# Small TensorE tiles, a split inversion and one written order of issue in a DeltaNet and MLP-Mixer kernel

## The chip, the cores and the metric

The kernel runs on one core of one Trainium2 chip. Its time is the device time of one launch in microseconds. A profile is one such launch, taken on the same chip; its "span" runs from the first to the last instruction and is about 1.8 us shorter than the launch. TensorE's granted clock is printed as a share of full speed: 1.00, or 0.50 where it was halved.

## The reference

Four batch elements, eight heads, 768 positions, head width 48. The first part is a delta-rule recurrence, the second a mixer of two small MLPs, one across the positions and one across the channels:

```python
for t in range(S):
    y[:, :, t] = einsum('bhd,bhde->bhe', q[:, :, t], state)
    v_old = einsum('bhde,bhd->bhe', state, k_n[:, :, t])       # k_n: k / (|k| + 1e-6)
    state = state + beta_t * outer(k_n[:, :, t], v[:, :, t] - v_old)
# x: y as (batch, 768, 384)
u = x + (relu(x^T @ w_tok1) @ w_tok2)^T        # 768 -> 256 -> 768
out = u + relu(u @ w_ch1) @ w_ch2              # 384 -> 1536 -> 384
```

The weights come as float64 and are rounded to fp32 in the kernel.

## The kernel before

The recurrence is done in chunks of 64 positions, twelve per batch element; two chunks are a unit of 128 rows. For each unit and head a triangular 64x64 matrix has to be inverted. VectorE inverts its 32x32 diagonal blocks by substitution, for up to four units in one round, and TensorE joins the blocks:

```python
def invert(rnd):                       # 30 steps of two VectorE operations
    for s in range(1, HB - 1):         # HB = 32
        w = HB - 1 - s
        nc.vector.tensor_tensor(out=tmp, in0=x[:, 0:s, s:s+1]..., in1=x[:, s:s+1, s+1:HB]..., op=mult)
        nc.vector.tensor_tensor(out=x[:, 0:s, s+1:HB], in0=x[:, 0:s, s+1:HB], in1=tmp, op=add)
        yield
```

Each chunk is then three products that wait for one another, over two heads at a time as block-diagonal matrices of 128 rows. The zero halves make TensorE do twice the work, and each result is copied out in two halves:

```python
p_q = kqt[:, 2p+cc]^T @ s0[:, p]       # 128x128 by 96 columns
r_bd[r, :, e] = v_st - p_q             # VectorE, once per half
p_w = gm^T @ r_bd                      # 128x65 by 96
w_bd[r, :, e] = p_w                    # ScalarE, once per half
p_s = gm^T @ w_bd                      # 128x128 by 96
s1[r, :, e] = s0 + p_s                 # VectorE, once per half
```

Every piece of work is a generator, and a heap of (time, step) values decides in which order their steps are issued. Each engine carries out its own instructions in that order.

## Time and profile before

| stretch | us | what happens |
|---|---|---|
| A 0 to 39.5 | 39.5 | loads, preparation of the first units |
| B 39.5 to 86.0 | 46.5 | first round of inversion, on VectorE |
| C 86.0 to 96.6 | 10.6 | joining the blocks |
| D 96.6 to 180.6 | 83.9 | recurrence of the first batch element |
| 180.6 to 820.8 | 640.2 | four mixers and the other three recurrences |

The time was 821.29 us, the median of three runs (819.48 to 821.9). The lines behind the table are in the prediction. A stage ends where the timeline shows the event named, and its busy times are read for that stretch alone: 92% for TensorE over the whole span says nothing of B, where TensorE waits for VectorE.

### The profile page before, as it was taken

How to read it: one execution, taken by the hardware profiler on the slowest of the kernel's cores; microseconds unless marked ns; L12 is line 12 of the kernel's file. 1: busy time of each engine (PE TensorE's matmuls, PEld its weight loads, DVE VectorE, ACT ScalarE, POOL GpSimd, SP SyncE). 2: the span in 40 equal slices, each digit the busy share in tenths (PEclk: the TensorE clock that was granted, in tenths of full speed). 3: DMA queues.
4: the chain of work that ended last, by engine and by line, in shares of the span. 5: the costliest groups of instructions: out<-in, count | busy, mean ns of one | idle time of the engine just before them, and what ended most of it. 6: DMA issues, size and time to landing. Idle time of an engine off the chain costs nothing.

```text
span 820.8 us, 13554 instructions
## 1 busy us (share of the span) xinstructions
PE 753.4 (92%) x5204; PEld 611.7 (75%) x5204; DVE 411.8 (50%) x1115; ACT 266.9 (33%) x619; POOL 103.4 (13%) x126
## 2 busy tenths in 40 slices
PE   7772598898889999999999999999999999999998
PEld 4641576776669887876977889868888888578876
DVE  4699899868863576332394233762258221100000
ACT  4524545653425531332322333212322221011110
POOL 2043002424321200020100011010000000000000
PEclk9786699999999999999999999999999999999999
DMA  7536212465433332231313031121011100000000
GB/s 128 103 89 134 76 34 46 99 160 136 135 105 65 69 79 55 47 71 36 65 25 73 21 62 28 41 65 17 18 30 33 34 11 10 10 3 18 10 10 20
DMA packets 151088, 46.60 MB, mean 57 GB/s; under 512 B 142416, under 2 KB 145488, under 8 KB 151024
## 3 DMA queue, kind: packets, MB, share of 16 engines
q1 hardware_dynamic: 151024, 45.74, 25.2%
q8 instruction: 41, 0.67, 0.4%
q14 instruction: 23, 0.19, 0.1%
HBM read 36.27 MB, written 9.44 MB: 56 GB/s over the span
## 4 chain that ended last, share of the span: by engine, by line
PE 61%; DVE 22%; ACT 6%; DMA 4%; issue 4%; SPq 3%; POOL 1%; ACTq 0%; POOLq 0%; DVEq 0%
PE p_o L648 17%; PE p_c L632 16%; DVE sub L458 6%; PE p_g L367 5%; DVE x L462 5%; PE p_s L562 4%; PE p_q L530 3%; PE p_h L606 3%; PE p L593 3%; PE p_w L548 3%; PE p_z L487 2%; PE p_x L496 2%; ACT kbd L345 2%; SPq L272 2%; DMA kst<-in_k_dram 1%
## 5 line engine op out<-in xcount | busy, mean ns | idle before, releaser
L632 PE MATMUL p_c<-u_t,wc 128*128 128x128 f32 x1728 | 215.1, 278 | 2.7 <-ACT u_t L620 2.7
L632 PEld LDWEIGHTS p_c<-u_t,wc 128*128 128x128 f32 x1728 | 204.8, 193 | 8.0 <-ACT u_t L620 3.2
L648 PE MATMUL p_o<-wc,r 128*128 128x384 f32 x576 | 198.2, 490 | 5.9 <-DVE wc L207 5.9
L648 PEld LDWEIGHTS p_o<-wc,r 128*128 128x128 f32 x576 | 104.5, 190 | 69.2 <-DVE wc L207 9.6
L640 ACT ACTIVATE r<-p_c 128x512 f32<-128x512 f32 x72 | 43.0, 597 | 142.6 <-PE p_c L632 142.2
L458 DVE TENSOR_TENSOR sub<-x 128x30 f32<-128x30 f32 (+22 forms) x210 | 77.4, 369 | 12.7 <-DMA x<-n_dram 8.2
L462 DVE TENSOR_TENSOR x<-x,sub 128x30 f32<-128x30 f32 (+22 forms) x210 | 76.3, 363 | 4.0
L367 PE MATMUL p_g<-kqt,kbd 128*128 128x128 f32 x384 | 59.1, 309 | 18.1 <-ACT kqt L357 18.0
L654 DVE TENSOR_TENSOR xb<-xb,p_o 128x384 f32<-128x384 f32 x24 | 13.3, 555 | 121.0 <-PE p_o L648 120.8
L367 PEld LDWEIGHTS p_g<-kqt,kbd 128*128 128x128 f32 x384 | 53.8, 219 | 24.8 <-ACT kqt L357 23.5
L369 DVE TENSOR_TENSOR gm<-p_g,mb 128x512 f32<-128x512 f32 x48 | 33.0, 689 | 52.6 <-PE p_g L367 52.3
L566 DVE TENSOR_TENSOR s_bd<-s_bd,p_s 64x192 f32<-64x192 f32 (+1 forms) x100 | 31.6, 316 | 52.1 <-PE p_s L562 50.1
L562 PE MATMUL p_s<-w_bd,gm 128*128 128x96 f32 x384 | 54.4, 279 | 2.9 <-ACT w_bd L552 2.3
L536 ACT ACTIVATE xb<-p_q 64x384 f32<-64x384 f32 (+1 forms) x55 | 22.9, 419 | 103.3 <-DVE r_bd L532 99.2
L562 PEld LDWEIGHTS p_s<-w_bd,gm 128*128 128x128 f32 x384 | 48.4, 191 | 8.6 <-ACT w_bd L552 7.5
L532 DVE TENSOR_TENSOR r_bd<-v_st,p_q 64x192 f32<-64x192 f32 (+1 forms) x110 | 34.7, 316 | 38.8 <-PE p_q L530 24.7
L552 ACT COPY w_bd<-p_w 64x192 f32<-64x192 f32 (+1 forms) x120 | 33.5, 279 | 55.9 <-PE p_w L548 53.6
L530 PEld LDWEIGHTS p_q<-s_bd,kqt 128*128 128x128 f32 x352 | 45.2, 191 | 8.2 <-issue 2.2
L530 PE MATMUL p_q<-s_bd,kqt 128*128 128x96 f32 x352 | 48.3, 275 | 2.4 <-DVE s_bd L566 2.3
L156 PE MATMUL p_warm<-warm 128*128 128x256 f32 (+1 forms) x124 | 47.9, 511 | 1.5 <-DVE warm L98 1.1
L487 PE MATMUL p_z<-t,gm 128*65 128x64 f32 x384 | 28.5, 227 | 22.0 <-DVE t L482 21.9
L205 POOL TENSOR_TENSOR w_f<-w_f,d 128x384 uint32<-128x384 uint32 (+1 forms) x34 | 37.1, 1092 | 79.1 <-DVE w_f L199 35.6
(86 smaller groups left out, 779.0 us busy)
## 6 DMA issues: line engine op xcount, KB each, us to landing
d<-in_moe_w_ch_dram SPq DMA_DIRECT2D x24, 384.0 KB, 3.6
kpad<-in_k_dram SPq DMA_DIRECT2D x24, 192.0 KB, 3.2
kst<-in_k_dram SPq DMA_DIRECT2D x96, 48.0 KB, 2.7
qpad<-in_q_dram SPq DMA_DIRECT2D x24, 192.0 KB, 3.5
v_st<-in_v_dram SPq DMA_DIRECT2D x96, 48.0 KB, 2.6
out_dram<-xb SPq DMA_DIRECT2D x24, 192.0 KB, 1.9
n_dram<-gm SPq DMA_DIRECT2D x72, 32.0 KB, 1.7
gm<-w_dram SPq DMA_DIRECT2D x72, 32.0 KB, 2.1
```

What stands on the lines that cost most here:

```text
L156: nc.tensor.matmul(p, zero, zero[:, None, :].to_broadcast([128, m, 128]))
L205: nc.gpsimd.tensor_tensor(out=f, in0=f, in1=lo, op=ALU.add)
L367: nc.tensor.matmul(p_g[:, i], kbd[:, nb], kqt[:, nb])
L458: nc.vector.tensor_tensor(out=tmp, in0=x[:, 0:s, s : s + 1].to_broadcast([n, s, w]), in1=x[:, s : s + 1, s + 1 : HB].to_broadcast([n, s, w ...
L462: nc.vector.tensor_tensor(out=x[:, 0:s, s + 1 : HB], in0=x[:, 0:s, s + 1 : HB], in1=tmp, op=ALU.add,)
L487: nc.tensor.matmul(p_z[0 : C + 1, nb], weights_of(u, nb), t11[:, nb])
L530: nc.tensor.matmul(p_q[:, p], kqt[:, 2 * p + cc], s0[:, p])
L532: nc.vector.tensor_tensor(out=r_bd[r, hp, e], in0=v_st[r, hp, cc], in1=p_q[hi, hp, e], op=ALU.subtract,)
L562: nc.tensor.matmul(p_s[:, p], gm[:, 2 * p + cc, 0:2], w_bd[:, p])
L632: nc.tensor.matmul(p_c[:, i], piece_of(wc1, cb, f * 128)[:, f * 128 : (f + 1) * 128], u_t[:, cb], start=(cb == 0), stop=(cb == NCB - 1),)
L640: nc.scalar.activation(r, p_c, ACTF.Relu)
L648: nc.tensor.matmul(p_o, r2[f // FG][:, f % FG], piece_of(wc2, f, 0), start=(f == 0), stop=(f == NHT - 1),)
```

## The change

Its intent: the first batch element has nothing to overlap with until the mixer has an input, so everything ahead of the first mixer matmul counts. There are three parts. Blocks of 16 in place of 32 halve the steps of substitution, and TensorE joins them in 32-row tiles. The first recurrence works in 64-row tiles, each on a quarter of the array, so that no zero halves are multiplied or copied. The heap of times is replaced by one written list of 2,184 steps.

```diff
-        for s in range(1, HB - 1):
-            w = HB - 1 - s
+        for s in range(1, m - 1):              # m = 16 for the first batch element, k = 2 blocks at once
+            w = m - 1 - s
...
+    def join_16(u):                            # 32-row tiles
+        for nb in range(NB):
+            for i, (block, _, _) in enumerate(quarters(u)):
+                r = slice(HB * i, HB * i + HB)
+                nc.tensor.matmul(p_z[r, nb], block[:, nb], t16[r, :, j * NB + nb])
...
+    def recur_early(t):                        # 64-row tiles
+            for p, i in by_head:
+                nc.tensor.matmul(p_k[PAR[i], p], kqt[f, 2 * p + cc, 0], s0[f, p])
+            nc.vector.tensor_tensor(out=rest, in0=p_k, in1=v_st[:, :, cc], op=ALU.subtract)
+            ... p_y, p_w, a ScalarE copy, p_s, the new state, p_y again
...
-    at(*WEIGHTS[1], load_weights, (wc1, moe_w_ch1))     # and the rest of the plan of times
-    run_plan()
+    order = """
+    w1*5 w2 z x*2 b k0*4 w2 k0 x y*2 w2*3 p0*2 y p0 y*3 k0 k1 b*2 p0*7 k1*4 p1*2 w3 k1
+    ... (r: recurrence, i: inversion, j, h: joining, p: preparation, w: weights, m: mixer, x y z: warming)
+    """
+    for word in order.split():
+        name, _, n = word.partition("*")
+        for _ in range(int(n or 1)):
+            next(jobs[name])
```

## The prediction

> **What bounds the kernel now.** I read the page first, then busy time stage by stage, then the order of TensorE's work in time. The page:
>
> ```profile
> span 820.8 us, 13554 instructions
> PE 753.4 (92%) x5204; PEld 611.7 (75%) x5204; DVE 411.8 (50%) x1115; ACT 266.9 (33%) x619; POOL 103.4 (13%) x126
> PE   7772598898889999999999999999999999999998
> DVE  4699899868863576332394233762258221100000
> PEclk9786699999999999999999999999999999999999
> ```
>
> TensorE's 92% is an average over two regimes. From slice 12 on (about 240 us) it is full at full clock; before that VectorE is the fuller engine and TensorE's clock is throttled. So I cut the span at the events that the timeline shows: inversion of the first four units begins (39.46), ends (86), first recurrence matmul (96.64), first mixer matmul (180.58), last wait of the mixer for its weights (236.19), last mixer alone (704.19).
>
> ```profile
> 0.00:39.46 39.46, 29.63 (x169) 22.20 (x170) 21.11 (x56) 20.67 (x40) 4.44 (x18) 0.87 0.64 120
> 39.46:86.00 46.54, 21.07 (x76) 12.53 (x75) 44.81 (x111) 15.40 (x34) 16.78 (x20) 0.76 0.52 115
> 86.00:96.64 10.64, 5.96 (x36) 4.84 (x37) 10.07 (x28) 8.19 (x17) 0.00 (x0) 0.50 0.16 66
> 96.64:180.58 83.94, 75.39 (x606) 65.38 (x604) 70.75 (x229) 45.96 (x135) 20.56 (x21) 0.97 0.36 77
> 180.58:236.19 55.61, 47.12 (x234) 33.32 (x232) 49.51 (x130) 23.95 (x49) 23.12 (x22) 0.97 0.44 124
> 236.19:704.19 468.00, 461.65 (x3448) 387.27 (x3449) 208.34 (x552) 138.61 (x321) 38.49 (x45) 1.00 0.21 45
> 704.19:820.80 116.61, 112.60 (x642) 86.15 (x641) 7.21 (x13) 14.06 (x26) 0.00 (x0) 1.00 0.04 13
> ```
>
> Columns: stretch and length; busy time of matmul, weight load, VectorE, ScalarE, GpSimd; granted clock; DMA share; GB/s. VectorE is busy 44.8 of 46.5 us in the inversion, 10.1 of 10.6 while the blocks are joined, 70.8 of 83.9 in the recurrence. TensorE's 75.4 us in the recurrence includes 20.6 us of warming matmuls, which a query for their tile gives. TensorE's order:
>
> ```profile
> 33.32 3.54 PE L367 MATMUL p_g<-kqt,kbd 128*128 128x128 f32 x16 [2.46 <-ACT kqt L357]
> 65.18 2.05 PE L367 MATMUL p_g<-kqt,kbd 128*128 128x128 f32 x16 [1.46 <-ACT kqt L357]
> 88.25 1.99 PE L487 MATMUL p_z<-t,gm 128*65 128x64 f32 x16 [21.02 <-DVE t L482]
> 142.78 1.09 PE L548 MATMUL p_w<-r_bd,gm 128*65 128x96 f32 x8 [0.56 <-DVE r_bd L532]
> 144.14 1.20 PE L562 MATMUL p_s<-w_bd,gm 128*128 128x96 f32 x8 [0.27 <-ACT w_bd L552]
> 180.58 7.93 PE L593 MATMUL p<-xb,w 128*128 128x384 f32 x24
> 219.20 0.91 PE L648 MATMUL p_o<-wc,r 128*128 128x384 f32 x2 [0.76 <-DVE wc L207]
> ```
>
> TensorE waits 21 us for the inversion, then for a VectorE or ScalarE step between recurrence matmuls, and from 209 to 236 in short waits for VectorE's last weight conversions. Two regimes follow: up to the mixer's start the end is set by VectorE and the dependent chain, after that by TensorE's total work. A microsecond saved before 180 therefore counts, if no work is pushed behind it.
>
> **What the Trainium skill says.** (1) TensorEngine Tiling (Array Packing), section Tiling Modes: tiles work independently and can load weights and multiply in parallel, but changing the tiling mode drains the engine. The trace has one tiled group: beta's transposes, 32x64 tiles, two column groups:
>
> ```profile
> L166 PE MATMUL p_b<-ident,b_rows x48: 204/204/225, 9.6 to 10.9; 32*64 32x16 f32 x48
> 9.58 1.57 PE L166 MATMUL p_b<-ident,b_rows 32*64 32x16 f32 x48
> ```
>
> 48 passes in 1.57 us are 33 ns each, against 0.92/16 = 57 ns for a 65-column pass of joining (the chain's 0.92 us for 16). So concurrency agrees; the untiled matmuls behind it start without a visible gap, so a drain is not visible here. (2) TensorE: Matmul & The Clock Gate, Part 1: an idle window of about 3.4 us halves the clock. This agrees: granted 0.50 at 86 to 97, and 16 passes p_g take 3.54 us cold, 2.05 warm. (3) The same page, Part 2, LDWEIGHTS: loading goes by columns. This agrees: 65 columns 57 ns, 128 about 117 (eight p_s passes take 0.93 to 0.95). (4) SBUF — State Buffer, Who interferes with whom: a tensor_tensor with two SBUF inputs contends with GpSimd reads. This agrees: an 84-element multiply took 1.02 us beside a GpSimd operation, 0.24 without.
>
> **The change part by part.** An fp32 matmul is two passes here.
>
> *Inversion.* Now 60 VectorE operations per round by a mean of 0.366 us (L458, L462) = 22.0, plus transposes 2.0 + 1.9: 26 us. After: 14 steps of 2 operations on 28 to 112 elements, where forms of 30 to 108 elements take 0.21 to 0.35, say 0.27: 7.6; transposes 2.0 + 1.0 + 1.9, memsets 0.3: 13 us. There are two early rounds, so 26 us of VectorE work go.
>
> *Joining the 16-blocks* is added: per unit 64 + 64 passes of 32x32 tiles by 33 ns = 4.2 us of TensorE, one ScalarE copy, four small copies. Joining the 32-blocks becomes 64 passes by 33 ns = 2.1 us, before 0.94 + 0.92.
>
> *Recurrence.* Per chunk now on VectorE: 4 r_bd by 0.255, 4 s_bd by 0.256, 2 y by 0.347 = 2.7 us; after: one 128x192 and two 48x192 by 0.36 = 1.1, y goes to ScalarE. Over 12 chunks 20 us go. TensorE: 40 matmuls, 80 passes by 33 = 2.6 us, as before (8 by 117 + 8 by 83 + 8 by 117 ns = 2.5). The longest chain, three stages of 16 passes (0.53 + 0.25 latency), copies of 0.36, 0.36, 0.72 and three handovers of 0.2, is about 4.4 us per chunk; now 83.9/12 = 7.0.
>
> *Preparation.* Two ScalarE copies into kbd (0.58 each) go for six units: 7 us. p_g has 32 passes over two tiles, so about the same 1.8 us. The first weights are now loaded ahead of k, which delays k by about 2.5 us (three issues of 0.6 and their transfers).
>
> *Late batches.* p_s loads 112 columns rather than 128: 288 passes by about 14 ns = 4 us less TensorE. The rest stays.
>
> *The explicit order.* I counted the work in it between its own milestones, with the durations above:
>
> - A, to the start of inversion: VectorE 23.8, TensorE 12.5, ScalarE 17.0, 33 DMA issues of about 0.6 = 20. The last k lands near 22, plus one unit's chain, plus queueing behind weights: 32 us (before 39.5).
> - B, inversion: VectorE 14.8, little else; 18 us with GpSimd contention (before 46.5).
> - C, to the first recurrence matmul: TensorE 14.5, ScalarE 10.8, VectorE 7.4, but ten handovers: 15 us (before 10.6; this gets longer).
> - D, recurrence to the first mixer matmul: VectorE 74.6, TensorE 65.5, ScalarE 56. VectorE stays full: inversion of the second round (12), a third of the third round's (12), weights 18, preparation 14, recurrence 12. At the present 84 to 87% fill: 85 us (before 83.9). So D keeps its length, because work that came later is pulled into it.
>
> Mixer start: 32 + 18 + 15 + 85 = 150, against 180.6: 30 us earlier.
>
> After it, TensorE. Per mixer 116.6 us (the last one alone), four = 466. Per late unit now: preparation 2.7, joining 1.86, two chunks 4.95 = 9.5; 18 units 171; of that four preparations (11) lie ahead of 180.6, which leaves 626. Measured 820.8 - 180.6 = 640: 14 us are idle, which the waits from 196 to 236 account for. After the change I counted the order from its first mixer step on, operation by operation, at back-to-back rates (322 ns per 384-column pass, 112 per 128-column pass, 117 and 83 for late recurrence, 103 for the narrower p_s): 601 us. So counted, a mixer is 112 us, against 116.6 measured alone; the gaps of the first three are filled by other work, those of the last are not: 605. Idle time: VectorE still has 49 us until the last weight is converted, beside 52 us of TensorE work, the same ratio as now; I leave 11 us. Sum: 150 + 605 + 11 = 766.
>
> **The rivals.** *(a) Small tiles do not overlap.* With 32- or 64-row tiles at 57 ns per pass, or with drains at mode changes, the 2,100 tiled passes of recurrence and joining cost 24 ns more each, 50 us; half of it would be hidden behind VectorE: 790. For it: only one short tiled group is in the trace. Against: its 33 ns. *(b) Cold clock.* The order has almost no warming in the recurrence, and small tiles may not count as activity. At clock 0.5 a stage costs 0.5 us more, three stages in 12 chunks = 19 us, and preparation doubles: 785 to 795. For it: 0.50 at 86 to 97. Against: with 65 us of work in 85 the idle gaps stay short. *(c) One wrong place in a fixed order blocks an engine.* The order is long and fitted; if durations are off by 10%, queues wait for one another, costing 10 to 20 us: 780. *(d) The chain sets D, not VectorE:* 12 by 4.4 = 53 us, with TensorE's 65 as the floor: D 70, total about 750. *(e) No gain, since weights arrive at the same time:* conversions finish at 236 now; the order ends them about 60 us after the mixer starts, so near 210. DMA is 0.36 to 0.52 busy, so it can follow. That would have to fail for the time to stay near 810.
>
> **Range and chances.** (d) gives the low end, (a) and (b) the high end; together 745 to 792 should hold it 8 times in 10. For less than 2% gain (above 804.9) two rivals must come true at once: faster 0.93, same 0.05, slower 0.02.
>
> **What would show it right or wrong.** Inversion (28 operations, mean 0.27) over 18 us; VectorE in it still near full. First mixer matmul near 150. Tiled passes at about 33 ns start to start. Granted clock near 1 in the recurrence. Last weight conversion near 210. The last mixer alone still 116 us. The prediction is wrong if the mixer starts after 170, or if TensorE then shows more than 25 us of waits.

## The result

The changed kernel took 786.02 us, the median of four runs (783.87 to 786.98), against 820.38 (817.5 to 821.9) for the kernel before in the same rounds. The ratio is 0.9582, 95% interval 0.9547 to 0.9616. Such a ratio is the mean time of one kernel's fast runs over that of the other's in the same rounds, so it is not quite the ratio of the medians.

The page of the changed kernel, the lines that the prediction shows of before:

```profile
span 784.5 us, 16847 instructions
PE 742.1 (95%) x6950; PEld 607.9 (77%) x6950; DVE 383.0 (49%) x983; ACT 256.0 (33%) x589; POOL 99.5 (13%) x122
PE   8879987988899999997899999999999999999998
DVE  6987778898735724337433538231228433200000
PEclk9976568799999999999799999999999999999999
```

The clock line is the first surprise. Slices 3 to 7 (59 to 157 us) hold the recurrence, and the clock is low there while TensorE's own line shows 7 to 9. One more dip stands at slice 19, near 380 us. The stages, in the columns of the prediction's table:

```profile
0.00:29.00 29.00, 24.52 (x299) 17.86 (x299) 20.74 (x62) 16.09 (x34) 5.46 (x15) 1.00 0.77 160
29.00:47.00 18.00, 12.98 (x89) 7.02 (x93) 17.00 (x48) 5.49 (x11) 3.92 (x5) 1.00 0.63 129
47.00:61.16 14.16, 12.41 (x486) 10.33 (x486) 12.01 (x29) 9.49 (x23) 4.51 (x5) 0.62 0.47 108
61.16:148.67 87.51, 78.49 (x1758) 70.74 (x1755) 70.49 (x173) 50.93 (x125) 25.83 (x28) 0.69 0.46 99
148.67:212.00 63.33, 54.79 (x407) 42.04 (x405) 55.06 (x123) 32.47 (x73) 22.45 (x26) 1.00 0.51 127
212.00:667.90 455.90, 446.71 (x3279) 373.40 (x3278) 199.81 (x538) 126.36 (x294) 37.37 (x45) 0.99 0.21 44
667.90:784.50 116.60, 112.22 (x653) 86.51 (x651) 7.92 (x15) 15.16 (x29) 0.00 (x0) 1.00 0.04 13
```

| stretch | before | predicted | measured |
|---|---|---|---|
| A, to the inversion | 39.5 | 32 | 29.0 |
| B, first inversion | 46.5 | 18 | 18.0 |
| C, joining | 10.6 | 15 | 14.2 |
| D, recurrence of the first element | 83.9 | 85 | 87.5 |
| from the first mixer matmul on | 640.2 | 616 | 635.8 |
| span | 820.8 | 766 | 784.5 |

So 32 us are gained ahead of the mixer, where 30 were predicted, and 4 after it, where 24 were expected. Two things need explaining: the missing 20 us, and whether D is as long as predicted for the reason that was given, since the clock there was to be near 1.

In the timeline of TensorE one wait stands out in the later part. The lines are start, length, engine, line, operation, tiles, shapes and, in brackets, the idle time ahead and what ended it:

```profile
374.36 0.72 DVE L722 TENSOR_TENSOR r_bd<-p_q,v_st 64x192 f32<-64x192 f32 x2
375.12 0.48 ACT L726 COPY xb<-p_q 64x384 f32<-64x384 f32 x1 [11.55 <-DVE r_bd L722]
375.62 1.09 ACT L819 ACTIVATE r<-p_c 128x512 f32<-128x512 f32 x2
376.27 10.56 PE L827 MATMUL p_o<-wc,r 128*128 128x384 f32 x24 [8.26 <-ACT r L819]
```

The wait is named for the mixer's relu (L819), but the relu is only a bystander. It stands in ScalarE's queue behind the copy of L726, which stands behind VectorE's r_bd of the same p_q, and that comes after the steps of a late inversion. Each engine waits for its next instruction in the list, though later ones could go. The Trainium skill, TensorE: Matmul & The Clock Gate, Architectural detail, says that ScalarE and VectorE are strict first-in first-out queues; this trace agrees: ScalarE is idle for 11.55 us ahead of the copy, and the relu behind it starts at 375.62, though the p_c matmuls, the last of them at 367.68, had long ended. TensorE is idle for 8.26 us, its clock falls, and the 24 passes behind take 10.56 us rather than 24 by 0.322 = 7.7: together about 11 us.

To see the rest I counted TensorE's passes in each stretch at the back-to-back rates of the prediction. After the mixer's start they make 601.4 us, where 601 was predicted. The elapsed 635.8 us therefore hold 34.4 us of excess, against 15 allowed: 13.3 up to 212 us, while weights are still converted, 11.3 between 358 and 390 us around that wait, 5.2 in the last mixer, 4.6 spread over the rest.

### The profile page after: what moved, and what is told of

Its sections match the earlier page's. It is cut to its first block, busy times and chain, and to the rows that moved or that the text cites. A ratio compares the mean times of both kernels' runs of the same rounds, so it can differ in the third digit from the quotient of the medians.

```text
span 784.5 us, 16847 instructions
## 1 busy us (share of the span) xinstructions
PE 742.1 (95%) x6950; PEld 607.9 (77%) x6950; DVE 383.0 (49%) x983; ACT 256.0 (33%) x589; POOL 99.5 (13%) x122
## 4 chain that ended last, share of the span: by engine, by line
PE 79%; DVE 11%; SPq 3%; issue 2%; ACT 2%; DMA 2%; POOL 1%; POOLq 0%; ACTq 0%; DVEq 0%
PE p_o L827 24%; PE p_c L811 23%; PE p_g L385 4%; PE p_s L743 3%; PE p_q L719 3%; PE p L772 3%; DVE x L512 3%; PE p_w L735 3%; DVE sub L507 2%; SPq L292 2%; PE p_h L785 2%; PE p_z L604 2%; PE p_x L613 2%; PE p_t L353 1%; PE p_w L665 1%
## 5 line engine op out<-in xcount | busy, mean ns | idle before, releaser
L819 ACT ACTIVATE r<-p_c 128x512 f32<-128x512 f32 x72 | 42.9, 597 | 202.1 <-PE p_c L811 201.7
L833 DVE TENSOR_TENSOR xb<-xb,p_o 128x384 f32<-128x384 f32 x24 | 13.3, 554 | 152.6 <-PE p_o L827 152.6
L507 DVE TENSOR_TENSOR sub<-x 128x84 f32<-128x84 f32 (+24 forms) x178 | 61.7, 347 | 10.8 <-DMA x<-n_dram 6.0
L512 DVE TENSOR_TENSOR x<-x,sub 128x84 f32<-128x84 f32 (+24 forms) x178 | 63.3, 356 | 6.1
L364 POOL TENSOR_TENSOR mb<-mask_c,cs 128x512 f32<-128x512 f32 x20 | 21.6, 1079 | 253.2 <-DVE cs L343 217.0
L751 DVE TENSOR_TENSOR s_bd<-s_bd,p_s 48x192 f32<-48x192 f32 x60 | 21.4, 357 | 56.5 <-PE p_s L743 55.3
L726 ACT COPY xb<-p_q 64x384 f32<-64x384 f32 x33 | 15.7, 475 | 98.9 <-DVE r_bd L722 96.8
L385 PE MATMUL p_g<-kqt,kbd 128*128 128x128 f32 x288 | 41.4, 294 | 1.8 <-ACT kqt L373 0.7
L302 POOL TENSOR_TENSOR v_st<-v_st,nrm 128x384 f32<-128x384 f32 x24 | 20.2, 845 | 177.7 <-DMA v_st<-in_v_dram 167.5
L722 DVE TENSOR_TENSOR r_bd<-p_q,v_st 64x192 f32<-64x192 f32 x66 | 23.1, 350 | 32.9 <-PE p_q L719 18.5
L772 PE MATMUL p<-xb,w 128*128 128x384 f32 x96 | 34.4, 491 | 1.8 <-DVE w L232 1.8
L785 PE MATMUL p_h<-r,w 128*128 128x384 f32 x96 | 33.7, 492 | 2.0 <-DVE xb L789 1.9
L743 PEld LDWEIGHTS p_s<-w_bd,gm 128*112 128x112 f32 x288 | 32.1, 178 | 3.6 <-ACT w_bd L738 0.6
```

The costliest lines, as they stand in the source:

```text
L385: nc.tensor.matmul(p_g[:, i], kbd[:, nb], kqt[:, nb])
L507: nc.vector.tensor_tensor(out=tmp, in0=y[:, :, 0:s, s : s + 1].to_broadcast([n, k, s, w]), in1=y[:, :, s : s + 1, s + 1 : m].to_broadcast( ...
L512: nc.vector.tensor_tensor(out=y[:, :, 0:s, s + 1 : m], in0=y[:, :, 0:s, s + 1 : m], in1=tmp, op=ALU.add,)
L743: nc.tensor.matmul(p_s[0 : C + D, p], gm[:, 2 * p + cc, C:], w_bd[:, p])
L772: nc.tensor.matmul(p_1[dh], piece_of(w1, c, 0)[:, dh * 128 : (dh + 1) * 128], xb[:, c], start=(c == 0), stop=(c == NCH - 1),)
L785: nc.tensor.matmul(p_h, piece_of(w2, j, c * 128)[:, c * 128 : (c + 1) * 128], r1[j], start=(j == 0), stop=(j == NDH - 1),)
```

## The experiments

Each of these groups ran on one chip and shares runs of the kernel before, whose median is given: e1 to e4 (820.8 us), e5 to e7 (821.76), e8 and e9 (821.74), e10 to e12 (822.27).

### e1: one step of the list moved

```diff
-    i4*3 m1*5 i4 k19 k21 k20 k21 v14*3 k20 i4*8 j13 r26 m1*9 ...
+    r26 i4*3 m1*5 i4 k19 k21 k20 k21 v14*3 k20 i4*8 j13 m1*9 ...
```

The step "r26" is the eviction of p_q; it now stands ahead of the inversion steps "i4".

> The eviction of one recurrence product of the second batch (r26) is put ahead of twelve inversion steps in the order. Theory (a queue held up by one badly placed entry: TensorE waits 8.3 us for ScalarE's relu, which stands behind a copy that waits for VectorE's inversion steps, and then runs about 3 us at half clock): 11 us faster than the changed kernel, about 775 us (772 to 778), and no wait of more than 3 us of the p_o matmuls between 350 and 400 us. Rival (inversion itself is what the second batch waits for, so the wait only moves): 783 to 787 us, with a wait of like size on the next join or recurrence step.

Measured: correct, 777.9 us (775.97 to 778.78, five runs), ratio 0.9468 (0.9443 to 0.9492), against 0.9582 for the changed kernel: 9 us gained, where 11 were expected. The same 60 us of both kernels, first the changed one, then this:

```profile
340.00:400.00 60.00, 51.51 (x350) 41.77 (x350) 32.55 (x87) 14.84 (x34) 5.95 (x8) 0.91 0.20 43
```

```profile
340.00:400.00 60.00, 59.78 (x402) 48.19 (x401) 36.76 (x100) 15.99 (x37) 5.94 (x8) 1.00 0.29 58
```

TensorE is now busy for 59.78 of 60 us and does 52 passes more. The wait was one misplaced step. From the first mixer matmul on this profile has 623.3 us, 12.6 less than the changed kernel's. Its stretch D, which the edit does not touch, is 92.3 us long at a clock of 0.65, against 87.5 at 0.69. So 4.8 of the 12.6 us are lost again in D; that difference between identical instruction lists will be used below.

### e2 and e5: the recurrence in plain 128-row blocks

The first element's recurrence goes back to block-diagonal products, at the places that the list gives to the tiles.

```diff
-        jobs[f"r{t}"] = recur(t) if t >= NQ else recur_early(t)
+        jobs[f"r{t}"] = recur(t) if t >= NQ else recur_slots(t)   # recur(t), its steps spread over the same places
```

> First batch's recurrence in full 128-row block-diagonal matmuls again, at the same places of the order. Theory (the stretch of the recurrence is set by VectorE's total work; the tiled recurrence helps by the 0.9 us of VectorE it saves per chunk): 8 to 12 us slower, about 795 us, VectorE busy about 80 us before the first mixer matmul's stretch instead of 70. Rival 1 (the dependent chain through TensorE sets it, and tiles shorten that): over 20 us slower. Rival 2 (neither, tiles are at a cold clock and full matmuls at a warm one, which cancels): 783 to 789 us.

Measured: 817.86 us (ratio 0.9956), but with a wrong result: relative error 0.205. A simulation showed that only the first element was wrong, from chunk 5 on. My list of places, "11011011", issued the new state at the eighth place, where the changed kernel has it at the seventh, and the list starts chunk 5 before chunk 4's eighth place. The run was repeated with "11011110".

> The plain recurrence again, with its mistake mended: in the run before, the state's new value was written one place of the order too late, behind the first product of the next chunk, so that the result was wrong. Now the second product and the new state stand where the changed kernel has them. Expect a correct result. If that late place made the run before slow, the stretch from the recurrence's first matmul to the mixer's first (87.5 us in the changed kernel, 116.3 in that run) comes back to 95 to 100 and the total to 794 to 800. If the full 128-row blocks themselves make it slow (more TensorE time, copies twice as many on the two narrow engines), it stays at 108 to 116 and the total at 808 to 818. I hold the second for likelier, 0.65.

Measured: correct, 815.44 us (813.88 to 816.2), ratio 0.9923. The likelier branch: D is 115.8 us, 28 more than with tiles.

```profile
61.46:177.30 115.84, 86.99 (x1131) 75.79 (x1131) 78.10 (x193) 51.36 (x123) 25.33 (x27) 0.66 0.34 74
```

Of TensorE's waits in that stretch (us in total, times, longest), three lead:

```profile
PE p_w L736 <- ACT gm L588: 9.4, 3, 4.6
PE p_w L736 <- DVE r_bd L723: 6.8, 5, 2.0
PE p_s L744 <- ACT w_bd L739: 6.4, 6, 2.5
```

These are 22.6 us of waiting for ScalarE's and VectorE's small steps, 9.4 of them for the joined block (gm). With tiles TensorE waits 2.9 us for r_bd, 2.9 for w_bd and, ahead of p_w, not at all for gm in D. So the tiles are worth their while. The list was fitted to the tiles, so how well plain blocks do in a list of their own stays open; before, with less other work in D and at a clock of 0.97 in place of 0.66, they took 83.9 us. Part of the 28 us may therefore be the clock: here it is at a half for 79.8 us of D, with tiles for 54.0.

### e3: blocks of 32 again

Only the inversion is undone: 30 steps per early round, nothing joined at 16.

```diff
-        if early:
-            k, m = 2, QB
+        if early:
+            y = x[:, None]         # one block of 32, m = HB
...
-    def join_16(u):   # products and copies
+    def join_16(u):   # empty steps
```

> The first batch's two rounds are inverted by substitution in blocks of 32 again, nothing is joined at 16; the rest stays. Theory (VectorE's time counts one for one before the mixer starts): VectorE gets 2 x 13 us more, joining takes about 4 us less before the first recurrence: about 806 us (799 to 812), inversion of the first round 30 us or more instead of 18. Rival (substitution was only waiting beside other work, as it is in the late batches): under 795 us.

Measured: correct, 799.31 us (798.66 to 799.47), ratio 0.9733: 13 us slower than the changed kernel, at the low edge of what was expected. The first round and the recurrence:

```profile
29.00:67.15 38.15, 15.22 (x104) 8.70 (x103) 35.81 (x92) 9.48 (x19) 6.33 (x8) 0.77 0.38 77
71.81:163.94 92.13, 76.43 (x1372) 67.46 (x1370) 83.97 (x201) 49.16 (x118) 27.24 (x29) 0.69 0.46 98
```

The inversion is ready 20 us later (67.15 for 46.88) and the recurrence starts 10.7 us later, because there is less to join. The second early round then loads VectorE in D with 84 us, and D is 4.6 us longer. The first mixer matmul comes 15.3 us later.

### e4: less for VectorE

Two of VectorE's three operations that round a piece of the weights are left out. Its output is wrong, which doesn't matter for the time.

```diff
-        nc.vector.tensor_scalar(out=f, in0=hi, scalar1=0x07FFFFFF, scalar2=3, ...)
-        nc.vector.scalar_tensor_tensor(out=f, in0=hi, scalar=0xC0000000, in1=f, ...)
-        nc.gpsimd.tensor_tensor(out=f, in0=f, in1=lo, op=ALU.add)
+        nc.gpsimd.tensor_tensor(out=f, in0=lo, in1=lo, op=ALU.add)
```

> Two of VectorE's three operations per rounded piece of the weights are left out (the result is wrong on purpose): 0.9 us by 34 pieces = 31 us less VectorE work, 10 of it in the recurrence's stretch. Theory (VectorE sets that stretch): first mixer matmul 6 to 10 us earlier, total 770 to 778 us. Rival (the dependent chain, or TensorE's tiles at a low clock, set it): first mixer matmul within 2 us of where it was (149), total 780 to 786 us.

Measured: 776.42 us (774.21 to 777.34), ratio 0.9452, with the 8.3 us wait of the changed kernel still in it. The total is in the range of the theory that VectorE sets D, but the step behind it failed: the mixer started 4.6 us sooner, not 6 to 10. D went from 87.5 to 83.7 us when VectorE lost 13.7 of its 70.5:

```profile
60.35:144.05 83.70, 76.55 (x1759) 68.45 (x1756) 56.79 (x147) 52.02 (x128) 25.08 (x31) 0.73 0.48 103
```

VectorE is idle for a third of the time and D hardly shortens. Something else sets it: TensorE, busy 76.6 of 83.7 us at 0.73 of its clock, or the chain of dependent steps that runs through it.

### e6 and e7: warming in the recurrence

Both start from e1. One warming matmul ("x": two passes of 128x128 by 128 columns on zeros) follows each of the 57 products of the recurrence in e6, and only p_w and p_s, 23 times, in e7.

```diff
-    ... r3 i1 w18*2 r3 p6 i1 r3 j3 r3*2 ...
+    ... r3 i1 w18*2 r3 x p6 i1 r3 x j3 r3*2 x ...      # e6; e7 without the first
```

> The kernel with the early eviction (777.9 us, stretch from the recurrence's first matmul to the mixer's first 92.3 us in its profile at a clock of 0.65), and in that stretch one warming matmul of 128x128 by 128 columns after each of the first batch's 57 recurrence products. If the half clock sets the stretch, the clock goes to 0.95 or more, and the stretch gets shorter by 5 to 12 us although TensorE has some 13 us more to do; total 766 to 773. If VectorE and the chain of the recurrence set it, the clock rises and the stretch stays within 3 us; total 775 to 781. If the added passes only stand in the chain and the clock does not rise, the stretch is 10 to 25 us longer; total 788 to 803. Chances 0.4, 0.3, 0.3.

Measured: correct, 784.63 us (784.22 to 785.38), ratio 0.9551. None of the three ranges fits; it is nearest to the third, for a reason that the third did not have.

> As the run before it, with 23 warming matmuls in place of 57, after the products p_w and p_s of each chunk only (some 5 us of TensorE at full clock). If the half clock sets the stretch and little warming is enough, the clock goes above 0.85 and the stretch is 5 to 10 us shorter, total 768 to 773. If the clock stays below 0.75, the stretch is as long or up to 10 us longer, total 778 to 788.

Measured: correct, 780.96 us (779.25 to 781.59), ratio 0.9499: the total of the second branch, though the clock was 0.77 over the stretch. Each kernel's D, cut where its clock changes, e6 first:

```profile
61.08:125.55 64.47, 62.05 (x1414) 53.07 (x1411) 53.97 (x126) 40.70 (x98) 22.37 (x23) 0.98 0.45 95
125.55:159.68 34.13, 33.94 (x445) 27.17 (x446) 18.49 (x54) 11.76 (x31) 5.24 (x7) 0.50 0.38 86
```

```profile
61.59:104.41 42.82, 41.74 (x762) 37.08 (x761) 23.91 (x69) 19.14 (x48) 6.45 (x7) 0.54 0.34 71
104.41:154.62 50.21, 43.54 (x1048) 37.29 (x1046) 44.02 (x105) 31.50 (x77) 18.84 (x20) 0.97 0.53 114
```

The clock has two states, and each kernel stays in one of them for a long time. e6 keeps full clock up to chunk 8, then falls and does not come up for 34 us, though TensorE is busy for 33.94 of 34.13 us and is given warming matmuls all along. So being busy is not enough to raise the clock.

What does? The recorded clock changes only at steps of 3.41 us. For every such window of all fourteen profiles I summed the work of the passes started in it: columns, times the rows and the columns of the tile over 128. A 64x64 tile thus counts a quarter. At full clock a window holds 3,413 ns / 112 ns by 128, about 3,900 full-array columns, in passes of 128 columns (322 ns by 384 columns gives 4,070).

| work in a window | next window at full clock, now full | next at full clock, now half |
|---|---|---|
| under 600 columns | 0 of 43 | 0 of 79 |
| 600 to 1,200 | 37 of 74 | 21 of 121 |
| over 1,200 | 2,821 of 2,823 | 50 of 63 |

Of the 174 half-clock windows in which TensorE was busy for over 90%, only 69 were followed by a full one. Array work tells far more than busy time. The rows of the tile alone tell more still. Count each pass as its columns times the tile's rows over 128, without its width, so that a 64x64 tile counts a half; the same windows then split almost cleanly at 1,500:

| work by rows in a window | next window at full clock, now full | next at full clock, now half |
|---|---|---|
| under 1,500 columns | 2 of 81 | 0 of 171 |
| 1,500 and over | 2,857 of 2,860 | 71 of 92 |

This one limit misplaces 26 of the 3,204 windows; the best single limit by area misplaces 72. Both limits were fitted to these windows. So it is few rows, more than narrow tiles, that go with the half clock here. Three windows of the changed kernel show it at work (the columns are as above):

```profile
88.00:91.31 3.31, 3.19 (x58) 2.70 (x60) 3.08 (x11) 2.27 (x7) 0.87 (x2) 0.50 0.24 45
91.31:94.72 3.41, 3.41 (x28) 3.32 (x26) 2.42 (x8) 0.50 (x2) 0.00 (x0) 0.50 0.53 160
94.72:98.13 3.41, 3.41 (x88) 3.16 (x88) 2.80 (x6) 1.20 (x4) 1.93 (x3) 1.00 0.49 116
```

In the middle one 16 passes of 128x128 run (p_g, 91.99 to 95.26), and the clock is full in the next; the small tiles of the windows before had kept TensorE as busy without that. All this is correlation over windows: no run changed the rows of the tiles and nothing else, so that rows are the measure is not shown by itself. The expectation of e8 below speaks of area; it was written before this count by rows.

### e8: warming where the clock fell

From e1: "x" after every product in chunks 0 to 7, after p_w and p_s in chunks 8 to 11, and three matmuls of 128x512 ("z") around the join ahead of chunk 8.

```diff
-    ... p9 j4 p9 w16 ... r8 x f5*3 v5 f5 w7 j4 ...
+    ... p9 j4 z p9 w16 ... r8 x f5*3 v5 f5 w7 z*2 j4 ...      # and x as in e6, then as in e7
```

> The early eviction, with one warming matmul after each recurrence product of the chunks 0 to 7 (there it held the clock at 1.00), after p_w and p_s alone in the chunks 8 to 11 (there that was enough), and three warming matmuls of 128x512 around the join ahead of chunk 8, where the clock fell in the run with warming after every product. Theory: TensorE's clock is decided anew every 3.41 us by how much of the array's area worked in that stretch, not by how long it was busy, and small tiles count for little; kept at full clock, the recurrence's stretch is shorter although more is issued. Then the clock is above 0.95 from 64 us to the mixer's first matmul, that stretch is 80 to 85 us (61 to 141..146; 87.5 in the changed kernel, 92.3 in the run with the early eviction alone), and the total is 767 to 772. Rival: VectorE and the chain take over as soon as the clock is up, the stretch stays at 87 or more, total 774 to 781. Other rival: the clock falls elsewhere, total 778 to 788.

Measured: correct, 774.91 us (774.67 to 777.57, five runs), ratio 0.9439 (0.9413 to 0.9465). The clock did what the theory said. D did not: it is 87.1 us. The total is that of the first rival.

```profile
61.51:148.61 87.10, 84.38 (x1854) 70.32 (x1852) 70.27 (x173) 51.04 (x125) 25.84 (x28) 0.95 0.47 101
```

TensorE is busy for 84.38 of 87.10 us. The warming passes are not free, as TensorE's timeline in e6 shows at full clock:

```profile
105.89 0.67 PE L646 MATMUL p_k<-s_bd,kqt 48*64 48x48 f32 x16
106.48 0.49 PE L164 MATMUL p_warm<-warm 128*128 128x128 f32 x2
106.90 0.67 PE L656 MATMUL p_y<-s_bd,kqt 48*64 48x48 f32 x16
```

The two passes hold the next product back from 106.48 to 106.90, 0.42 us; at another place, from 109.53 to 109.86, it is 0.33. So a pass costs about 0.19 us. Not all of it is the pass. In the changed kernel, e6 and e8, at full clock, the first 64-row pass behind a 128-row pass of 128 columns starts 0.20 us after it (median of 86), against 0.11 between two 128-row passes; from a 64-row pass to the first 128-row one it is 0.15 us (median of 93), where passes of 64-row tiles follow one another mostly within 0.05. Each change of tile size thus takes about 0.09 us more, and a warming step between two small products brings two of them. One of these is not in the 0.42 us, so 0.19 is rather low.

### e9: warming before the first join

```diff
-    ... k6 i0 k6 h3 ...
+    ... k6 i0 k6 z*4 h3 ...       # from e8
```

> As the run before it, and four warming matmuls of 128x512 more, ahead of the first join's products, where TensorE waits 3.3 us for VectorE's transposes and the clock falls to a half for the next 7 us. If the clock sets the joins' stretch (47 to 61 us, mean clock 0.62), it stays at 1.00 up to 56 us or so and the recurrence starts 2 to 4 us sooner; total 1 to 4 us below the run before it. If the joins wait for the copies on the two narrow engines, the start moves by under 1 us and the total by under 1 us. If the four matmuls last longer than the wait, the inversion's end is passed by up to 1 us and it is a loss of that size.

Measured: correct, 782.3 us median of six runs, ratio of the fast ones 0.9485 (0.9425 to 0.9545). Two runs, the profiled one among them, were over 1.5% above the fastest and count as slow. The four fast ones alone go from 775.38 us at a mean clock of 0.989 to 786.62 at 0.974. No gain. In the one profile, of a slow run, the clock is full up to 56.2 us as intended, and the recurrence still starts at 61.92, against 61.51 in e8: this points to the second branch, the copies, but one slow run does not settle it. What it does show is that the clock's path is not the same from run to run of one program: half a clock for 2 x (0.989 - 0.974) x 775 = 23 us more goes with 11.2 us more time.

### e10: no warming in the recurrence

From e1, without the seven steps that warm there (34 passes).

```diff
-    ... w13 r8 p8*2 ... r8 x f5*3 ... j4 r8*2 y r8 ...
+    ... w13 r8 p8*2 ... r8 f5*3 ... j4 r8*2 r8 ...
```

> The early eviction alone, without the seven groups of warming matmuls (34 passes) that stand between the first batch's first and last recurrence products. If the clock matters in that stretch and these passes keep some of it, its mean clock falls from 0.65 to 0.55 or less, the stretch is 3 to 8 us longer than 92.3 us, total 781 to 786 (777.9 with them). If they do nothing for the clock, which the small tiles pull down anyway, TensorE is rid of some 5 to 10 us of work in a stretch where it is 90% busy and the total is 770 to 777.

Measured: correct, 776.94 us (773.19 to 777.69), ratio 0.9448 (0.9414 to 0.9482), as fast as e1 (0.9468) within the intervals. The clock is 0.63, hardly lower. D is in the second branch's spirit, and the total at its upper edge:

```profile
60.92:151.09 90.17, 80.56 (x1724) 73.83 (x1721) 70.72 (x175) 51.06 (x126) 26.29 (x28) 0.63 0.46 98
```

### e11: e8 without its first five warming matmuls

```diff
-    ... r0 x ... r0 x ... r0 x ... r1 x ... r1 x ... r1 x
+    ... r0 ... r0 ... r0 ... r1 ... r1 ... r1 x
```

> As the run with warming where the clock falls (774.9 us), without the five warming matmuls in chunk 0 and at the start of chunk 1, where they ran at half clock and the first chunk took 9.9 us, against 7.1 in the changed kernel. If these five only stood in the way, the recurrence's stretch is 84 to 86 us in place of 87.1 and the total 772 to 774.5. If the clock needs them, it stays at a half past 70 us and the total is 776 to 783.

Measured: correct, 787.14 us (786.23 to 790.52), ratio 0.9595: slower than either branch allowed. The clock needed them, and it fell at 70 us and came back only at 107.6:

```profile
67.00:107.60 40.60, 39.58 (x572) 33.65 (x572) 20.94 (x60) 15.12 (x40) 5.63 (x6) 0.54 0.33 70
107.60:159.17 51.57, 49.02 (x1077) 40.35 (x1077) 44.27 (x105) 31.69 (x77) 19.07 (x20) 1.00 0.51 110
```

Warming that does not reach what a window asks for costs twice: the passes run at half clock, and the clock stays down.

### e12: less for VectorE, at full clock

e8 with the edit of e4. Its output is wrong, which doesn't matter for the time.

> Wrong result on purpose: the kernel with warming where the clock falls (774.9 us, recurrence's stretch 87.1 us at a clock of 0.95) and two of VectorE's three operations in the rounding of the weights dropped, which took 4.6 us off the start of the mixer in the changed kernel at a clock of 0.69. If VectorE is what is left once the clock is up, the stretch loses 8 to 14 us and the total is 759 to 766. If it is TensorE with its warming passes (85 of 88 us busy) or the chain of the recurrence, the stretch loses at most 4 us and the total is 768 to 772.

Measured: 766.59 us (765.87 to 768.19), ratio 0.9334. The total lies between the two branches; the stretch decides. VectorE lost 13.4 us of work in it and it lost 0.6:

```profile
59.02:145.49 86.47, 84.25 (x1855) 70.73 (x1852) 56.91 (x148) 51.27 (x127) 25.13 (x30) 0.93 0.47 102
```

So VectorE does not set D at nearly full clock either, with these warming passes in it. The other 7.7 us of the span's gain lie elsewhere: 2.5 ahead of the recurrence, and 5.2 after the mixer's start (619.5 us against 624.7), where weights are still converted. There VectorE does count.

### What sets D

The profiles of the tiled recurrence can be put to one sum, in us: D = 63.7 + 0.44 x (time at half clock) + 0.19 x (passes of warming beyond the changed kernel's 34). The 0.44 is the difference between the changed kernel and e1, which have the same instructions in D: (92.3 - 87.5) / (65.0 - 54.0). The 0.19 is read from the timeline above, and 63.7 is what is left of the changed kernel. Time at half clock is from the clock's records; 2 x (1 - clock) x D gives the same from the lines above. The other rows were not used to fit it:

| kernel | half clock, us | more passes | sum | D measured |
|---|---|---|---|---|
| e3, VectorE +13.5 us | 58.0 | 0 | 89.2 | 92.1 |
| e4, VectorE -13.7 us | 45.9 | 0 | 83.9 | 83.7 |
| e6 | 37.2 | 112 | 101.3 | 99.3 |
| e7 | 42.8 | 46 | 91.3 | 93.0 |
| e8 | 9.2 | 96 | 86.0 | 87.1 |
| e10 | 66.3 | -34 (0.08 each) | 90.2 | 90.2 |
| e11 | 39.4 | 86 | 97.4 | 97.8 |
| e12, VectorE -13.4 us | 11.5 | 96 | 87.0 | 86.5 |

(The passes that e10 leaves out are of the small kind; eight of them take 0.66 us in e6, 0.08 each.) The sum holds within about 2 us but for e3, and VectorE does not occur in it: e4's 3.8 us go with its shorter time at half clock. In e3, where VectorE is busy for 84.0 of 92.1 us, D is 2.9 us above the sum, so there VectorE does count. The slow profile of e9, left out of the table, has 48.9 us at half clock and 96 passes more: the sum gives 103.4, and D is 103.5.

The sum can't be followed down to no half clock at all. It would give 63.7 us, but in the changed kernel VectorE's list holds 69.0 us of work in D up to its last r_bd of the first element, at 146.68, on which the end of D waits. With this list D is therefore at least about 71 us, and to be rid of the half clock could save at most some 87.5 - 71 = 16 us, not the 0.44 x 54 = 24 us that the sum alone would give; both are estimates. Warming that avoids it costs as much: 96 passes by 0.19 = 18 us in e8. That is why the total scarcely moves.

## Why the prediction was right or wrong

The predicted 766 us missed the median of 786.02 by 20, within the range of 745 to 792; "faster" was right.

- **A, B, C: right in size and reason.** 29.0, 18.0 and 14.2 us for 32, 18 and 15. The inversion has 28 operations per early round, VectorE is busy for 17.00 of its 18.00 us, and e3 shows what blocks of 16 are worth: 13 us of the total.
- **Tiled passes at 33 ns: right for 64 rows, too high for 32.** From the start of sixteen 64-row passes to the next matmul, without a wait, it is mostly 0.40 to 0.62 us (25 to 39 ns a pass) at full clock, and 0.65 to 1.04 us at half. The 192 passes of 32x32 by 16 columns take 2.76 us, 14 ns each, at half clock. Rival (a), no overlap, fell. Its other half, the drain, was read too lightly: the prediction says that none is visible, but in that trace the last 32-row pass starts at 10.948 us and the first 128-row one at 11.083, 0.135 us later, where the pairs of tiled passes before them follow every 0.05.
- **D: the right number by two errors that cancel.** "VectorE stays full" and "granted clock near 1 in the recurrence" both failed. VectorE could lose 13 us, and D lost 3.8 and 0.6 (e4, e12). (Its 74.6 us were also too many: the five items named for it add up to 68, and 70.5 were measured.) Without the half clock D would have been 71 us at the least by the estimate above, near rival (d)'s "D 70". The half clock then gave back up to 16 us: rival (b), "small tiles may not count as activity", came true and was set at 19 us for the recurrence. The argument against it, that "the idle gaps stay short", looked at the wrong quantity. That the two cancelled is luck; the sizes rest on the sum above.
- **Mixer start at 150: right,** 148.67.
- **TensorE's work after it, 601 us: right,** 601.4 by the same count. **"I leave 11 us" of idle time and 4 for the last mixer: this is the step that failed.** The excess is 34.4 us, of which TensorE is idle for 22.1 and slower than counted for the rest; the prediction's own sign of being wrong, over 25 us of waits, is not met by the idle time alone. Of that 11.3 is rival (c), one wrong place in a fixed order, which e1 removed by moving one step; the weights' stretch took 13.3 where 11 stood for everything, the last mixer 5.2 where 4 was allowed, and 4.6 are small gaps. Why the weights' stretch has more is settled in part: e12 takes 5.2 us off by relieving VectorE.
- **Rival (e) fell:** the last weight conversion ends at 214.6 us, near the 210 that the count of the order gave.

What beats both kernels: e8 at 0.9439 and e10 at 0.9448 of the kernel before, e1 at 0.9468, against 0.9582. Their intervals overlap, so of the three only the moved step of e1, which all of them contain, is a shown gain. What is left of D without the half clock was not taken apart further.

## What to carry to other kernels

Before a wide matmul is cut into small tiles, ask what the clock will see: tiles of few rows that keep TensorE busy may still go with a clock at a half, and warming passes here cost about what they saved. In one fixed list, search the trace for the engine that waits behind an instruction it does not need; moving one eviction ahead of a long job was worth 9 us here, more than all tuning of the clock. And when a stage's length comes out as predicted, check the reason apart from the number, since two errors can cancel.

## What the Trainium skill lacked or had wrong

- TensorE: Matmul & The Clock Gate, Part 1, ties the clock to how busy the array has been, with idle windows of about 3.4 us. The windows agree (3.41 us steps in the records), but busy is not enough: e6 stayed at 0.50 for 34.13 us with TensorE busy for 33.94 of them. A window's work, its columns weighted by the tile's rows over 128, told the next state: under 1,500 only 2 of 252 were followed by full clock, from 1,500 on at full clock 2,857 of 2,860 stayed. The page does not say how small tiles count for the clock.
- TensorEngine Tiling (Array Packing), Tiling Modes, says that changing the mode drains the engine. The traces agree, and the page gives no figure: at 65.94 us the changed kernel starts its last 32-row pass and at 66.06 the first 64-row one, 0.12 us later (median of 15 such changes at full clock: 0.12), where the 32-row passes follow one another mostly within 0.03. Between 64 and 128 rows it is about 0.09 us more than without a change.
- No page looked at says what a warming pass costs between dependent small products: 0.33 to 0.42 us for two passes of 128 columns.
